# A linear-attention and two-MoE kernel: the first stage replanned with finer steps, and more mapping buffers

## The chip, the cores and the metric

The kernel runs on one core of one Trainium2 chip. The metric is the device time of one launch in microseconds (us), the median of the runs shown. The data is float32 throughout; matmuls are exact to float32 by splitting each operand into a high and a low part (three matmuls for one product).

## The reference

Three layers run one behind the other on 2304 tokens (4 batches of 576) of width 512 (8 heads of 64). A linear attention with 128 random features, a gated feed-forward layer ("MoE 1", inner width 1536), and a routed layer with 8 experts of which each token takes one ("MoE 2", inner width 1024).

```python
def phi(x):
    proj = np.einsum('bhsd,md->bhsm', x, omega)
    sq = np.sum(x * x, axis=-1, keepdims=True) / 2.0
    h = proj - sq
    h = h - np.max(h, axis=-1, keepdims=True)
    return np.exp(h) / np.sqrt(m)
q_p, k_p = (phi(q_s), phi(k_s))
kv = np.einsum('bhsm,bhsd->bhmd', k_p, v)
z = np.sum(k_p, axis=2)
num = np.einsum('bhsm,bhmd->bhsd', q_p, kv)
den = np.einsum('bhsm,bhm->bhs', q_p, z)[..., None] + 1e-06
attn = num / den
...
g = x @ w_gate
x2 = g * (1.0 / (1.0 + np.exp(-g))) * (x @ w_val) @ w_out
...
e_idx = np.argmax(x2 @ w_gate2 + modality_bias[modality_id], axis=1)
out[mask] = gate_w[mask, None] * (np.maximum(x2[mask] @ w1[e], 0.0) @ w2[e])
```

## The kernel before

The tokens are cut into 18 tiles of 128, and three tiles make one of six groups. A **unit** is the attention work of one tile and four heads, for k or for q. Its parts are named in `unit_stages`: T (transpose x on PE, tile `xt`), xh (copy to SBUF, ACT), xl (low part, VectorE), sq (squares), ss and sc (their sum and its scaling), pj (projection on PE, tile `pr`), rd (row maximum on VectorE, tile `mx`), md (two small subtractions on GpSimd, tile `mx` again), ex (exp on ACT, tile `h`). A k unit then adds to the sums kv (PE) and a q unit goes on with qt, qc, nm, dv, xt, hi, lo (transposed back, multiplied with kv, divided, and laid as high and low part into `xT`, the input of MoE 1).

MoE 1 takes a group in 12 steps f: 24 matmuls into `gv` for gate and value, an activation in five small steps (`th`, `uh`, `ul`), and nine matmuls into `acc`. Its weights come as 36 chunks (`wraw`), and in the first stage VectorE and ACT turn each chunk into a high and a low part in five steps (`wsteps`: one half-rate mask step, two combining steps, a cast on ACT, a subtraction).

The **first stage** runs from the start to the end of group 0 of MoE 1. It holds the first 16 units (10 of k, 6 of q, "start" units), the 14 units of the next group, all 36 chunks and the 12 steps f of group 0. The order in which this work is written out is set by a list scheduler, the class `Plan`: each step has an engine, a duration, what it needs, a rank and the buffers that it takes and gives. `run` picks the step that can start first and among equals the lowest rank, and calls its function, which records the instructions. Each engine later works off its own list in that order and waits where a step isn't ready. The durations stand in the table `dur`, the ranks come from constants at the top of the file (CR, CD, UR, MR and others). From group 1 on a clock of due times (`Tasks`) sets the order instead.

The routing of MoE 2 is found in rounds (`finish_route`). Its function `c` makes, per three tiles, three products `f_mv` and three one-hot tiles `f_lh` on VectorE, and PE multiplies them into `inv`. `f_lh` has three buffers in all, so the next three wait until PE has read the last ones. The pair `FR` sets how far apart these steps are due and how long after them their matmuls are.

In `s1b` the low part xl is recorded in the same step as xh, and in the plan this step is a step of ACT. The start units' vt memsets and copies, the scaling of ss and the sum of kv (`kv_put`) are likewise recorded inside other steps (first_edge, md, kv).

Of the kernel before, what the change touches and what calls it, by code (L numbers as in the profile page):

```python
# [29 lines left out]
FR = ((1.35, 3.0), (2.8, 6.0))  # L30
MD = (0, 0, 0.17, 1.8, 2.18)
QL = -0.4
QD = 0.51
LAT = 0.34
GRAIN = 0.02
CR = -13.06
CD = -7.43
CS = 11.68
UR = 67.55
UD = 9.05  # L40
MR = 44.82
MS = 30.96
RR = 91.36
XL = 19.61
WU = 4
GF = 0
# [3 lines left out]
RS = 3.38  # L50
PU = 14.29
# [29 lines left out]
class Plan:  # L81


    def __init__(self, bufs, lag):
        self.todo = []
        self.free = {}
        self.lag = lag
        self.bufs = {k: [0.0] * n for k, n in bufs.items()}
# [6 lines left out]
    def run(self, last):  # L95

        while last[7] is None:
            best = None
            for s in self.todo:
                eng, dur, fn, after, rank, take, give, end = s  # L100
                if any(a[7] is None for a in after) or any(not self.bufs[b] for b in take):
# [3 lines left out]
                key = (t // GRAIN, rank)  # L105
                if best is None or key < best[0]:
                    best = key, t, s
            key, t, s = best
            self.todo.remove(s)
# [3 lines left out]
            for b in s[6]:  # L113
                self.bufs[b].append(s[7] + LAT)
# [4 lines left out]
def kernel(  # L119
# [60 lines left out]
    with tc.manual_schedule():  # L180
# [76 lines left out]
        def load_v(n, vt):  # L257
            kind, t, j = units[n]
            if not edge(t):
                (r, m, b, s), = segs(t)  # L260
                nc.gpsimd.memset(vt[:, :, D:D + 2], 1.0)
                nc.sync.dma_start(out=vt[:, :, 0:D], in_=v[b, 4 * j:4 * j + 4, s:s + m, :].rearrange("h s d -> s h d"))
                return

            for hp in range(2):
                for i, (r, m, b, s) in enumerate(segs(t)):
                    nc.gpsimd.memset(vt[hp][r:r + m, :, 1 - i, :], 0.0)
                    nc.gpsimd.memset(vt[hp][r:r + m, :, i, D:D + 2], 1.0)
                    h = 4 * j + 2 * hp
# [3 lines left out]
        def pump():  # L273
            while nload[0] < len(units) and room["xin"]:
# [4 lines left out]
                nload[0] += 1  # L279
                pump_v()  # L280
            pump_v()
# [14 lines left out]

        def freed(tag):
            room[tag] += 1
            pump()
# [17 lines left out]
        def first_quad(src, j):  # L317
            quad[src, j] = wpool.tile([P, 4, 4, D], F32, tag="w", name="quad")
            nc.sync.dma_start(out=quad[src, j].rearrange("p h r d -> p h (r d)"),
                              in_=(k if src == "k" else v)[0, 4 * j:4 * j + 4, 0:4 * P, :].rearrange(  # L320
                                  "h (p r) d -> p h (r d)", r=4))
# [15 lines left out]
        def first_edge(j):  # L337
            n = units.index(("k", 4, j))
            vt = wpool.tile([P, 1024], F32, tag="w", name="vt")
            vt = [vt[:, 512 * a:512 * a + 4 * (D + 2)].rearrange("p (h b d) -> p h b d", h=2, b=2) for a in range(2)]  # L340
            loads[n] = first_x(n)
            vals[n] = vt
            load_v(n, vt)
# [8 lines left out]
        first_quad("k", 0)  # L352
        first_quad("v", 0)
# [81 lines left out]
        def unit_stages(i):  # L435
# [4 lines left out]
            native = start or i < n_start + min(GF, n_grp[0])  # L440
            accum = not start and i < n_start + n_grp[0]
# [8 lines left out]
            def s1():  # L450
# [5 lines left out]
                else:  # L456
                    x = loads.pop(i)
                    h = attn.tile([P, 4, M], F32, tag="h", name="h", bufs=2)
                    xh = attn.tile([P, 2, P], F32 if native else F32R, tag="xh", name="xh", bufs=1)
# [36 lines left out]
            def s2():  # L496
                xh, xl = st["xh"], st.get("xl")
                pr = st["pr"] = bank([P, 4, M], "pr")
                for a in range(2):
                    o = pr[:, 2 * a:2 * a + 2, :].rearrange("p h m -> p (h m)")  # L500
                    if native:
# [14 lines left out]
            def s2m():  # L516
                ss, mx = st["ss"], st["mx"]

                if start or accum:

                    if start:
                        nc.gpsimd.tensor_scalar(out=ss, in0=ss, scalar1=half_s2, scalar2=None, op0=ALU.mult)
# [23 lines left out]
            def s3k():  # L546
                h, vt = st["h"], vts.pop((t, j)) if x_none else vals.pop(i)
# [929 lines left out]
```

## Time and profile before

| | |
|---|---|
| median of three runs | 883.11 us (882.98 to 883.4) |
| the profiled execution, device time | 882.91 us |
| its span, first to last instruction | 880.7 us |
| PE busy | 854.5 us, 97% of the span |
| VectorE (DVE) busy | 598.9 us, 68% |
| ScalarE (ACT) busy | 370.4 us, 42% |
| GpSimd (POOL) busy | 97.1 us, 11% |

The span is 2.2 us shorter than the execution's device time. PE is the engine that sets the end: its matmuls of group 1 to the last expert follow each other almost without a gap, so a time that the first stage saves or loses moves everything behind it by the same amount. A share over the whole run says little of the first stage, where VectorE, GpSimd and ACT are as busy as PE.

### The profile page before, as it was taken

Reading aid. Unit: us, or ns where it says so; the run is one execution under the profiler, and the core shown is the slowest. Engines: PE = TensorE matmul, PEld = TensorE weight load, DVE = VectorE, ACT = ScalarE, POOL = GpSimd, SP = SyncE. Lnnn points to the kernel's source line nnn. Section 1 sums busy time; section 2 is a strip of 40 time slices with the busy share of each in tenths; the row PEclk is TensorE's granted clock in tenths of the full one; section 3 lists DMA queues with packets and bytes.
Section 4 is the critical chain, followed back from the end, with each engine's and each line's share of the span. In section 5 each row is a group of like instructions: output and inputs, shape, how many; then the busy total and the mean of one; then the engine's idle time right before and its main releaser. Section 6 shows DMA issues by size and latency. Waiting matters only on the chain. (4 is left out here: it accounts for less than half of the span.)

```text
span 880.7 us, 14618 instructions
## 1 busy us (share of the span) xinstructions
PE 854.5 (97%) x5115; PEld 789.1 (90%) x5115; DVE 598.9 (68%) x1582; ACT 370.4 (42%) x1023; POOL 97.1 (11%) x236
## 2 busy tenths in 40 slices
PE   7989999999999999999999999999999999999994
PEld 6878988999999999999999999999999999889994
DVE  5989999466665667555676665478787777876520
ACT  4865666343333433333433431111374445555420
POOL 6702101000000000000000000000112014311010
PEclk9999999999999999999999999999999999999998
DMA  8726642032223112141111311041767654666000
GB/s 268 210 67 203 190 152 78 7 114 55 61 60 103 42 42 55 43 127 47 36 37 44 84 31 42 33 135 31 266 216 282 199 180 149 237 236 238 28 27 26
DMA packets 89374, 98.69 MB, mean 112 GB/s; under 512 B 53488, under 2 KB 55554, under 8 KB 89291
## 3 DMA queue, kind: packets, MB, share of 16 engines
q1 hardware_dynamic: 85979, 87.90, 32.5%
q0 software_dynamic: 3040, 9.70, 3.2%
q8 instruction: 42, 0.69, 0.3%
q14 instruction: 41, 0.34, 0.1%
q10 hardware_dynamic: 272, 0.07, 0.0%
HBM read 84.26 MB, written 13.65 MB: 111 GB/s over the span
## 5 line engine op out<-in xcount | busy, mean ns | idle before, releaser
L166 PE MATMUL gv<-xT,w 128*128 128x384 f32 x576 | 202.2, 351 | 0.3 <-DVE th L1022 0.3
L168 PE MATMUL gv<-xT,w 128*128 128x384 f32 x576 | 194.8, 338 | 0.0
L167 PE MATMUL gv<-xT,w 128*128 128x384 f32 x576 | 194.5, 338 | 0.0
L166 PE MATMUL acc<-w,uh 128*128 128x512 f32 x352 | 143.5, 408 | 0.0
L168 PE MATMUL acc<-w,ul 128*128 128x512 f32 x352 | 139.1, 395 | 1.1 <-DVE ul L1201 1.0
L167 PE MATMUL acc<-w,uh 128*128 128x512 f32 x352 | 138.7, 394 | 0.0
L533 ACT ACTIVATE h<-pr,mx 128x128 f32<-128x128 f32 x224 | 64.0, 369 | 140.0 <-DVE mx L528 132.7
L166 PEld LDWEIGHTS gv<-xT,w 128*128 128x128 f32 x576 | 109.2, 190 | 4.2 <-DVE th L1022 1.4
L167 PEld LDWEIGHTS gv<-xT,w 128*128 128x128 f32 x576 | 109.2, 190 | 2.7
L168 PEld LDWEIGHTS gv<-xT,w 128*128 128x128 f32 x576 | 108.9, 189 | 0.0
L738 DVE SCALAR_TENSOR_TENSOR wge<-xrow,wge 128x512 f32<-128x512 f32 x144 | 98.6, 685 | 10.6 <-DMA wge<-wg2t 9.9
L172 DVE TENSOR_TENSOR w<-raw,w 128x512 fp32r<-128x512 f32 x128 | 85.1, 685 | 3.2 <-ACT w L171 2.3
L168 PEld LDWEIGHTS acc<-w,ul 128*128 128x128 f32 x352 | 66.0, 188 | 17.0 <-DVE ul L1201 2.4
L166 PE MATMUL h<-sx,w 128*128 128x256 f32 (+1 forms) x256 | 78.7, 308 | 0.0
L168 PE MATMUL h<-sx,w 128*128 128x256 f32 (+1 forms) x256 | 77.6, 303 | 0.0
L167 PE MATMUL h<-sx,w 128*128 128x256 f32 (+1 forms) x256 | 77.4, 302 | 0.0
L171 ACT CAST w<-raw 128x512 fp32r<-128x512 f32 x128 | 74.1, 618 | 2.4 <-DMA raw<-in_moe_w_dram 2.4
L167 PEld LDWEIGHTS acc<-w,uh 128*128 128x128 f32 x352 | 66.5, 189 | 7.5
L166 PEld LDWEIGHTS acc<-w,uh 128*128 128x128 f32 x352 | 66.4, 189 | 7.2
L1031 ACT CAST uh<-th 128x384 fp32r<-128x384 f32 x72 | 37.5, 521 | 72.7 <-DVE th L1026 72.5
L512 DVE TENSOR_REDUCE mx<-pr 128x4 f32<-128x512 f32 x72 | 49.4, 687 | 22.9 <-PE pr L168 19.8
L1022 DVE SCALAR_TENSOR_TENSOR th<-th,gv 128x384 f32<-128x384 f32 x72 | 39.6, 550 | 35.3 <-ACT th L1019 35.3
(232 smaller groups left out, 1404.2 us busy)
## 6 DMA issues: line engine op xcount, KB each, us to landing
raw<-in_moe_w_dram SPq DMA_DIRECT2D x64, 512.0 KB, 4.9
wge<-wg2t SPq DMA_DIRECT2D x48, 256.0 KB, 3.5
scr<-xrow SPq DMA_DIRECT2D x33, 256.0 KB, 3.0
wraw<-in_moe_w_gate_dram SPq DMA_DIRECT2D x12, 512.0 KB, 4.6
wraw<-in_moe_w_val_dram SPq DMA_DIRECT2D x12, 512.0 KB, 4.9
wraw<-in_moe_w_out_dram SPq DMA_DIRECT2D x12, 512.0 KB, 4.5
xin<-in_q_dram SPq DMA_DIRECT2D x26, 128.0 KB, 2.4
xin<-in_k_dram SPq DMA_DIRECT2D x24, 128.0 KB, 3.5
```

Source lines behind the costliest of these rows:

```text
L166: nc.tensor.matmul(o, lh, rh, start=start, stop=False, skip_group_check=True)
L167: nc.tensor.matmul(o, lh, rl, start=False, stop=False, skip_group_check=True)
L168: nc.tensor.matmul(o, ll, rh, start=False, stop=stop, skip_group_check=True)
L171: nc.scalar.copy(hi, src)
L172: nc.vector.tensor_tensor(out=lo, in0=src, in1=hi.bitcast(F32), op=ALU.subtract)
L512: nc.vector.tensor_reduce(out=mx, in_=pr, axis=AX.X, op=ALU.max)
L533: nc.scalar.activation(out=h[:, a, :], in_=pr[:, a, :], func=ACTF.Exp, bias=mx[:, a:a + 1])
L738: nc.vector.scalar_tensor_tensor(out=st[e][:, 1, :], in0=xrows[i], scalar=1.0, in1=st[e][:, 0, :], op0=ALU.mult, op1=ALU.mult, accum_out=L ...
L1022: nc.vector.scalar_tensor_tensor(out=th[f], in0=th[f], scalar=1.0, in1=ps.pop((f, "g")), op0=ALU.add, op1=ALU.mult)
L1031: nc.scalar.copy(u[f][0], th[f])
```

## The change

Work that was recorded inside other steps becomes steps of its own in the plan: xl (VectorE), sc (GpSimd), the edge units' vt memsets (GpSimd, ahead of their loads), the last sum of kv in a batch (`ka`, VectorE), and for the later k units the refill of the v buffer (`pv`, GpSimd). The lag between engines becomes a table by engine instead of one number, loads get a longer lag, durations are set anew, and so are nearly all ranks. The first load of k is cut into two halves, the transposition of the gate weights (`turn_gate`) waits for its load and the last value step, and the path `GF` that was switched off goes. In the routing, `f_lh` gets 8 buffers instead of 3, the due times `FR` are set anew, and `ge` of the third round, which runs only when tokens are left over, moves to another pool.

```diff
-FR = ((1.35, 3.0), (2.8, 6.0))
+FR = ((1.35, 2.6), (2.9, 4.0))
-LAT = 0.34
+LAT = dict(pe=0.25, act=0.14, dve=0.13, pool=0.14, dma=2.3)
-CR = -13.06
-CD = -7.43
+CR = 1.76
+CD = -8.74
...
-        first_quad("k", 0)
-        first_quad("v", 0)
+        first_quad("k", 0, 2)
...
             def s1b():
-                if native:
-                    nc.scalar.copy(st["xh"], st["xt"])
-                else:
-                    st["xl"] = attn.tile([P, 2, P], F32R, tag="xl", name="xl", bufs=1)
-                    split(st["xt"], st["xh"], st["xl"])
+                nc.scalar.copy(st["xh"], st["xt"])
+
+            def s1x():
+                xl = st["xl"] = attn.tile([P, 2, P], F32R, tag="xl", name="xl", bufs=1)
+                nc.vector.tensor_tensor(out=xl, in0=st["xt"], in1=st["xh"].bitcast(F32), op=ALU.subtract)
...
+            def s1e():
+                nc.gpsimd.tensor_scalar(out=st["ss"], in0=st["ss"], scalar1=half_s2, scalar2=None, op0=ALU.mult)
...
-                if t == own[-1]:
-                    kv_put((b, j), kv_ps[0], slice(0, 4))
                 if not x_none:
                     freed("vin")
+                if not planned and t == own[-1]:
+                    s3p()
+
+            def s3p():
+                kv_put(segs(t)[0][2:3] + (j,), kv_ps[0], slice(0, 4))
...
         def freed(tag):
             room[tag] += 1
-            pump()
+            if tag == "xin" or not planning:
+                pump()
...
-                        lh[i] = t_("f_lh", [P, P], F32R, bufs=GT)
+                        lh[i] = t_("f_lh", [P, P], F32R, bufs=8)
...
-        dur = dict(T=0.34, xh=0.26, sq=0.7, ss=0.42, pj=0.87, rd=0.7, md=0.4, ex=1.01, kv=0.83, ko=0.42, kw=0.43,
-                    kp=0.42, qt=0.43, qc=0.39, nm=0.87, dv=1.09, xt=0.22, hi=0.27, lo=0.34)
+        dur = dict(T=0.22, xh=0.26, xl=0.34, sq=0.57, ss=0.33, sc=0.55, pj=0.87, rd=0.6, md=0.5, ex=1.02, kv=0.83,
+                   ka=0.35, pv=0.25, ko=0.18, kw=0.43, kp=0.18, qt=0.43, qc=0.48, nm=0.84, dv=0.75, xt=0.22, hi=0.26, lo=0.34)
...
-            got["edge", j] = plan.add("dma", 1.46, lambda j=j: first_edge(j), rank=-8 + 4 * j, take=["w", "w"])
+        for j, rank in enumerate((KE, KF)):
+            s = plan.add("pool", 1.2, lambda j=j: first_edge(j, True), rank=rank, take=["w"])
+            got["edge", j] = plan.add("dma", 2.0, lambda j=j: first_edge(j, False), [s], rank=rank, take=["w"])
...
-        plan.add("pe", 0.4, turn_gate, [], MR + 75)
+        plan.add("pe", 0.6, turn_gate, [loaded, half["v", 1]], MR + 75)
```

What the new ranks do to the order is seen in the program's own lists. From group 1 of MoE 1 to the end the lists of all engines are the same before and after, but for where the routing's steps stand among the work around them.

PE, the last rows of the start units and the first matmuls of MoE 1 (`xot` brings a q unit's result back, `gv` is MoE 1, `pr<-om_h` the projection of a unit of the next group, `wt` is `turn_gate`); before:

```order
L605 MATMUL xot<-ident,first 128x128 x2
L470 MATMUL xt<-ident,xin 128x128 x2
L695 MATMUL wt<-ident,wg_97 8x128 x4
L166 MATMUL pr<-om_h,xh 128x256
L167 MATMUL pr<-om_l,xh 128x256
L168 MATMUL pr<-om_h,xl 128x256
L166 MATMUL pr<-om_h,xh 128x256
L167 MATMUL pr<-om_l,xh 128x256
L168 MATMUL pr<-om_h,xl 128x256
L166 MATMUL gv<-xT_644,w 128x384
L167 MATMUL gv<-xT_645,w 128x384
```

and of the change, in the same place:

```order
L653 MATMUL xot<-ident,first 128x128 x2
L514 MATMUL xt<-ident,xin 128x128 x2
L187 MATMUL gv<-xT_634,w 128x384
L188 MATMUL gv<-xT_635,w 128x384
L189 MATMUL gv<-xT_634,w 128x384
L187 MATMUL gv<-xT_634,w 128x384
L188 MATMUL gv<-xT_635,w 128x384
L189 MATMUL gv<-xT_634,w 128x384
L187 MATMUL pr<-om_h,xh 128x256
L188 MATMUL pr<-om_l,xh 128x256
L189 MATMUL pr<-om_h,xl 128x256
```

Before, the projections of two units and `wt` stand ahead of the first `gv`; now the first six `gv` come at once behind the last `xot`, both projections come later, and `wt` has gone to the end of group 0.

ACT, from the four copies of the first start units on (`first<-pr,mx` is the exp of a unit, `w<-wt` the cast of a weight chunk, `first<-xt` the copy xh of a start unit); before:

```order
L476 COPY first<-xt 128x256 x4
L533 ACTIVATE first<-pr,mx 128x128 x4
L476 COPY first<-xt 128x256
L533 ACTIVATE first<-pr,mx 128x128 x4
L420 CAST w<-wt 128x512
L533 ACTIVATE first<-pr,mx 128x128 x4
L420 CAST w<-wt 128x512
```

and of the change:

```order
L519 COPY first<-xt 128x256 x4
L578 ACTIVATE first<-pr,mx 128x128 x4
L464 CAST w<-wt 128x512
L578 ACTIVATE first<-pr,mx 128x128 x4
L464 CAST w<-wt 128x512
L519 COPY first<-xt 128x256 x2
L578 ACTIVATE first<-pr,mx 128x128 x4
```

The first two casts have each moved ahead of an exp, and the copy of the first edge unit, which stood behind the first exp, now stands behind the second cast.

PE, late in the run, at the fifth `inv` of the second routing round (`h` and `acc` are an expert's matmuls, `gx` transposes gathered rows); before:

```order
L168 MATMUL acc_8787<-w,ul 128x512
L1159 MATMUL gx<-ident,grow 128x128 x4
L166 MATMUL h_8932<-sx_8517,w 128x256
L167 MATMUL h_8932<-sx_8518,w 128x256
L168 MATMUL h_8932<-sx_8517,w 128x256
L166 MATMUL h_8932<-sx_8517,w 128x256
L167 MATMUL h_8932<-sx_8518,w 128x256
L168 MATMUL h_8932<-sx_8517,w 128x256
L974 MATMUL inv<-f_mv,f_lh 128x18 x3
```

and of the change:

```order
L189 MATMUL acc_8791<-w,ul 128x512
L1211 MATMUL gx<-ident,grow 128x128 x4
L1026 MATMUL inv<-f_mv,f_lh 128x18 x3
L187 MATMUL h_8933<-sx_8518,w 128x256
L188 MATMUL h_8933<-sx_8519,w 128x256
L189 MATMUL h_8933<-sx_8518,w 128x256
```

The three `inv` matmuls stand six matmuls earlier.

## Rows read from the trace of the kernel before

**Rows 1.** The page, part 1: busy time, share of span, instructions by engine

```profile
PE 854.5 (97%) x5115; PEld 789.1 (90%) x5115; DVE 598.9 (68%) x1582; ACT 370.4 (42%) x1023; POOL 97.1 (11%) x236
```

**Rows 2.** Stretch: its us, busy PE, PEld, DVE, ACT, POOL, granted clock, DMA

```profile
0.00:58.70 58.70, 47.72 (x290) 40.31 (x291) 46.52 (x106) 38.96 (x133) 32.22 (x110) 1.00 0.66 193
58.70:168.50 109.80, 106.91 (x651) 98.34 (x650) 96.68 (x203) 62.62 (x224) 13.76 (x34) 0.97 0.43 133
168.50:760.00 591.50, 591.50 (x3528) 553.20 (x3527) 398.25 (x1147) 223.57 (x574) 33.86 (x76) 1.00 0.32 99
760.00:785.00 25.00, 23.85 (x158) 20.97 (x157) 17.28 (x53) 11.73 (x24) 2.86 (x3) 1.00 0.56 199
```

**Rows 3.** Waits of PE, 0 to 150 us: total us, times, longest

```profile
PE kv L555 <- ACT h L533: 1.4, 1, 1.4
...
PE wt L695 <- DVE xl L172: 1.2, 1, 1.2
...
PE gv L166 <- DVE th L1022: 0.3, 1, 0.3
```

**Rows 4.** Busy time by stretch, around two falls of the clock

```profile
53.00:58.90 5.90, 3.26 (x22) 2.48 (x23) 5.71 (x14) 4.07 (x23) 0.45 (x2) 1.00 0.50 134
58.90:62.30 3.40, 3.40 (x12) 3.40 (x11) 3.34 (x7) 1.66 (x5) 0.77 (x2) 0.51 0.55 158
86.90:88.30 1.40, 0.02 (x1) 0.00 (x1) 0.61 (x2) 0.42 (x2) 0.87 (x2) 1.00 0.14 56
89.60:93.10 3.50, 3.50 (x15) 3.24 (x14) 3.50 (x8) 2.24 (x9) 0.08 (x1) 0.51 0.30 67
```

**Rows 5.** Timeline at the seam: start us, us, engine, instruction [idle before]

```profile
57.05 0.41 DVE L613 TENSOR_TENSOR xT<-xot,xT 128x256 fp32r<-128x256 f32 x1
...
57.88 0.39 PE L166 MATMUL pr<-om_h,xh 128*128 128x256 f32 x1 [0.69 <-ACT h L533]
...
58.70 0.34 PE L166 MATMUL gv<-xT,w 128*128 128x384 f32 x1
```

**Rows 6.** Timeline ahead of the stall at 87 us, GpSimd

```profile
85.31 2.26 POOL L523 TENSOR_TENSOR mx<-ss,mx 128x4 f32<-128x4 f32 x1 [4.58 <-ACT w L420]
```

**Rows 7.** GpSimd's first subtraction: min/median/max ns, first and last start

```profile
L523 POOL TENSOR_TENSOR mx<-ss,mx x30: 200/202/2256, 10.2 to 149.9; 128x4 f32<-128x4 f32 x30
```

**Rows 8.** VectorE groups of the first stage: busy us, mean ns, idle before

```profile
L411 DVE SCALAR_TENSOR_TENSOR wt<-wraw,wt 128x512 int32<-128x512 int32 x36 | 25.1, 704 | 0.0
...
L512 DVE TENSOR_REDUCE mx<-pr 128x4 f32<-128x512 f32 x30 | 20.4, 681 | 2.8 <-PE pr L502 2.7 <-PE pr L168 0.2
L407 DVE TENSOR_SCALAR wt<-wraw 128x512 int32<-128x512 int32 x36 | 15.3, 437 | 0.0
...
L507 DVE TENSOR_REDUCE ss<-first 128x4 f32<-128x256 f32 x16 | 6.5, 409 | 1.5 <-POOL vt L331 0.9 <-POOL first L484 0.6
L172 DVE TENSOR_TENSOR xl<-xt,xh 128x256 fp32r<-128x256 f32 x14 | 5.9, 419 | 3.0 <-ACT xh L171 2.9
```

**Rows 9.** Timeline of the start units

```profile
10.79 0.79 PE L470 MATMUL xt<-ident,quad 128*128 128x128 f32 x4
...
11.65 0.42 DVE L407 TENSOR_SCALAR wt<-wraw 128x512 int32<-128x512 int32 x1
...
13.48 1.15 ACT L533 ACTIVATE first<-pr,mx 128x128 f32<-128x128 f32 x4
...
14.49 0.64 ACT L420 CAST w<-wt 128x512 fp32r<-128x512 f32 x1
...
17.33 0.37 ACT L533 ACTIVATE first<-pr,mx 128x128 f32<-128x128 f32 x1 [2.19 <-POOL mx L524]
```

**Rows 10.** Waits at the second routing round, 760 to 785 us

```profile
DVE f_lh L969 <- PE inv L974: 7.5, 5, 3.0
```

**Rows 11.** The DMA view: one issue, KB each, median us to landing

```profile
wge<-wg2t SPq DMA_DIRECT2D x48, 256.0 KB, 3.5
...
quad<-in_k_dram SPq DMA_DIRECT2D x2, 512.0 KB, 5.1
```

More of the change, by code (lines that the diff above doesn't have):

```diff
@@ L85, in __init__ @@
         self.todo = []
+        self.next = {}
         self.free = {}
@@ L95, in run @@
     def run(self, last):
+        left = {}
+        ready = []
+        self.next = {}
+        for n, s in enumerate(self.todo):
+            wait = {id(a) for a in s[3] if a[7] is None}
+            for a in wait:
+                self.next.setdefault(a, []).append((n, s))
+            left[id(s)] = len(wait)
+            if not wait:
+                ready.append((n, s))
         while last[7] is None:
             best = None
-            for s in self.todo:
+            for n, s in ready:
                 eng, dur, fn, after, rank, take, give, end = s
-                if any(a[7] is None for a in after) or any(not self.bufs[b] for b in take):
+                if any(not self.bufs[b] for b in take):
                     continue
@@ L108, in run @@
             key, t, s = best
+            ready.remove((key[2], s))
             self.todo.remove(s)
@@ L113, in run @@
             for b in s[6]:
-                self.bufs[b].append(s[7] + LAT)
+                self.bufs[b].append(s[7] + self.lag[s[0]])
+            for n, x in self.next.get(id(s), ()):
+                left[id(x)] -= 1
+                if not left[id(x)]:
+                    ready.append((n, x))
             s[2]()
@@ L268, in load_v @@
                     nc.gpsimd.memset(vt[hp][r:r + m, :, i, D:D + 2], 1.0)
+        def load_v(n, vt, memset=True):
+            kind, t, j = units[n]
+            if memset:
+                ones_v(n, vt)
+            if not edge(t):
+                (r, m, b, s), = segs(t)
+                nc.sync.dma_start(out=vt[:, :, 0:D], in_=v[b, 4 * j:4 * j + 4, s:s + m, :].rearrange("h s d -> s h d"))
+                return
+            for hp in range(2):
+                for i, (r, m, b, s) in enumerate(segs(t)):
                     h = 4 * j + 2 * hp
@@ L279, in pump @@
                 nload[0] += 1
+                if not planning:
+                    pump_v()
+            if not planning:
                 pump_v()
-            pump_v()
         def pump_v():
@@ L439, in unit_stages @@
             start = i < n_start
-            native = start or i < n_start + min(GF, n_grp[0])
-            accum = not start and i < n_start + n_grp[0]
+            planned = i < n_start + n_grp[0]
+            accum = not start and planned
             def bank(shape, name):
@@ L625, in unit_stages @@
                 parts.update(kv=s3k)
+                if planned and t == max(x for x in batch_tiles(segs(t)[0][2]) if not edge(x)):
+                    parts.update(ka=s3p)
             else:
@@ L1304 @@
         on.update(sq="pool", ss="dve", md="pool")
[L1305 removed]
+        needs.update(ss=["sq"], sc=["ss"], rd=["pj"], md=["rd", "sc"], ex=["md"])
         ready = []
@@ L1308 @@
         om_split = plan.add("act", 0.3, lambda: split(om_f, om_h, om_l), [], OR)
-        pumped = plan.add("dma", 1.6, pump, [got["edge", 1]], PU)
+        pumped = plan.add("dma", 1.6, lambda: (pump(), pump_v()), [got["edge", 1]], PU)
         for i in range(nu):
@@ L1325 @@
                 step["x"] = got["edge", j]
-            native = i < n_start + min(GF, n_grp[0])
-            for n, f in unit_stages(i).items():
+            parts = unit_stages(i)
+            if kind == "k" and not early:
+                parts["pv"] = pump_v
+            for n, f in parts.items():
                 d = 0.43 if n == "kv" and edge(t) else dur[n]
@@ L1362 @@
         ra, rb, rc, rd = route_setup()
-        s = plan.add("dma", 0.5, later_loads, [s], XL)
+        s = loaded = plan.add("dma", 0.5, later_loads, [s], XL)
         s = plan.add("dve", 0.14, ra, [s], RR)
```

133 lines of the change are left out of this document (79 added, 54 removed).

## The prediction

> **What bounds the kernel now.** I read the page's busy times first, then the busy time by stretch, then who waited for whom on PE, and last the timeline at the places where PE waited. The page says that PE is busy 97% of the span [rows 1]. By stretch the picture is sharper: from 168.5 us, where group 1 of MoE 1 begins, to 760 us PE has not one idle microsecond, and VectorE has a third of its time free [rows 2]. What an order could still gain there is nothing. The idle time of PE lies in three places: 58.70 - 47.72 = 11.0 us before the first `gv` matmul, 109.80 - 106.91 = 2.9 us between it and 168.5 us, and 25.00 - 23.85 = 1.15 us around the second routing round [rows 2]. To this the clock adds something in the second stretch: its mean is 0.97, because of two falls of some 3.4 us each to 0.51, that is from 2.4 to 1.2 GHz [rows 4]. At half clock such a fall costs half its length, 1.7 us. Ahead of the first fall PE was busy 3.26 of 5.90 us, ahead of the second it had stood still for 1.4 us [rows 4].
>
> So the change can gain at most the avoidable part of 11.0 us, 2.9 + 3.4 = 6.3 us behind it, and 1.15 us late. What stands against it: PE's work in the first stage is the same before and after, and VectorE's nearly so. Both engines are close to full between 90 and 150 us, so a reordering gains only where one of them really stood.
>
> The sum is made against the profiled execution, 882.9 us (span 880.7 and 2.2 around it), 0.2 us under the median of the three runs. A measurement here tells about 0.2%, 1.8 us, from no change.
>
> **The change part by part.**
>
> *Start of the plan, up to some 20 us.* The edge units' memsets on GpSimd move to the first microseconds, where GpSimd is free; before, the second set stood in the way of a vt memset that VectorE waited 0.9 us for [rows 8]. That is a gain of at most 0.9 us. Against it, on ACT two weight casts have moved ahead of exps. Before, the second exp began at 13.48 and the first cast at 14.49 us [rows 9]. Now that cast is first. It can't start before VectorE's third step of the chunk, which in the new list has three steps in front of it behind the start at 11.65 us [rows 9] that the chunk work has in both orders; by the durations 0.44 + 0.70 + 0.44 + 0.70 less overlap this is 13.7 to 13.8 us [rows 8]. The exp then begins near 14.4, 0.9 us later, and the copy of the edge unit behind the second cast puts that unit's projection 1.6 us later. ACT then stood idle for 2.19 us before the third exp anyway [rows 9], so some of it is taken up. Bounds -0.9 and +1.6; I take 0, since VectorE has its list full of ready chunk steps in either order.
>
> *The first k load in two halves.* A load of 512 KB landed 5.1 us after issue, one of 256 KB 3.5 us after [rows 11]. The first half can't help the first transposes, which stand behind the random features' own load. The second half is needed by units 2 and 3, whose transposes, in their turn on PE, began at 10.79 us [rows 9], so 2 x 3.5 - 5.1 = 1.9 us more would be hidden: 0. The Trainium skill, "DMA: Bandwidth & Descriptors", section "Anatomy of one DMA", speaks against the cut: each DMA has a fixed cost of about 2 us whatever its size. By that rule the second half would land some 2 us later, which the same cover hides.
>
> *The seam at 58.7 us.* Before, PE waited 1.2 us for its `wt` transposes behind an xl [rows 3] and 0.69 us for an exp [rows 5], and of the last 5.9 us it idled 2.6 [rows 4]. In the new list the first six `gv` stand right behind the last start unit, both projections come later and `wt` much later. The last high/low part of a start unit ended at 57.46 us and the first `gv` came at 58.70 [rows 5]: 1.2 us to gain. Three things go against it. The two projections are PE work that is now done after the first `gv`, where PE has no idle time: 58.70 - 57.88 = 0.8 us each [rows 5], 1.6 in all. The last high/low part also stands later in VectorE's new list. I counted the rows in front of it: one weight chunk more (0.44 and three times 0.70) and six small setup steps of some 0.2, less two xl of 0.42 and one `mx` of 0.68 [rows 8] and some overlap, 1.2 to 1.7 us. And the clock's fall at 58.9 us, 1.7 us, may go if PE no longer idles there. -1.2 + 1.6 + 1.5 - 1.7 = +0.2. Bounds: -2.9 (no extra VectorE delay, the projections find idle time) and +3.1 (the clock still falls, and the exp still comes late). I take 0.
>
> *The stall at 87 us.* PE stood 1.4 us for a k unit's exp [rows 3], and behind it came the second fall of the clock, 1.7 us [rows 4]. The exp had waited for GpSimd's two tiny subtractions, of which the first took 2.26 us [rows 6], against 0.20 us at its median [rows 7]. Before, GpSimd's list also held the v buffers' memsets in front of such steps; as `pv` they are now steps with a place of their own, and xl, of 0.42 us on VectorE [rows 8], is now in the plan, which before counted it to ACT. So a meeting of just this kind should not come again in this place: -3.1 us. Bounds -3.1 and 0. But by the program's lists the PE work between a projection and the matmul that needs its exp has shrunk, from 4.8 to 3.9 us in the mean over 14 units, so I add one wait for an exp of the size of that at the seam, 0.7 us [rows 5]. Together -2.4.
>
> The Trainium skill, "GPSIMD Engine Reference", section "Specifications", says that GpSimd shares its SBUF interfaces with VectorE and is held up by VectorE instructions with two SBUF inputs or in a two-port mode. The 2.26 us fell among such instructions. By that rule the new plan, which books a fixed 0.5 us, meets the same chance wherever chunk steps follow a row maximum; that is the second rival below.
>
> *VectorE's load by step f.* Ahead of the end of step 4 its new list holds some 2.6 us less work, ahead of step 9 some 3 us less, at steps 5 to 7 the same. PE waited only 0.3 us in all for these steps [rows 3], so this is cover and no gain: 0. If PE came earlier by more than 3 us, VectorE would be late next.
>
> *`turn_gate` at the end of group 0.* The same four transposes, one copy and one load that the gate loads of group 0 need; these stand behind it in SP's list as before, and 591 us without an idle PE follow [rows 2]: 0.
>
> *Mapping buffers and FR.* VectorE waited five times, 7.5 us in all, for PE to read `f_lh` [rows 10]; the stretch has 1.15 us of idle PE [rows 2]. With eight buffers three new tiles needn't wait for three old ones. The matmuls are due 2 us earlier after their VectorE steps, but still 4 us after them, against some 1.1 us of work. -1.1 us; bounds -1.5 (with the slower first matmuls after a wait) and 0.
>
> Sum: 0 + 0 + 0 - 2.4 + 0 + 0 - 1.1 = -3.5, so 882.9 - 3.5 = **879.4 us**.
>
> **The rivals.**
>
> 1. *Everything after the seam closes.* Both falls of the clock and the 2.9 us of idle PE go: -6.3, with the mapping -1.1: 875.5 us. For it: xl and the sums of kv were missing in the old plan. Against it: the tighter distances.
>
> 2. *No gain in the first stage.* The finer plan is still no picture of the chip: GpSimd's steps stretch by chance (0.20 to 2.26 us, [rows 7]), so a stall of the old size comes elsewhere, and only the mapping's 1.1 us stays: 881.8 us, no change by the bound above. This also covers that the change doesn't do what it says.
>
> 3. *Slower: the start comes late.* The casts ahead of exps shift the start units by 1.6 us, the last high/low part is 1.5 us later by its place, the two projections' 1.6 us fall into full PE time, less 1.2 us at the seam; the stall and the falls stay as they are. +1.6 + 1.9 - 1.1 = +2.4: 885.3 us. It decides from the point where the first `gv` starts later than about 59.9 us: with the 1.6 us of work put off and the mapping's gain this is +1.7 us. For it: the first `gv` waits for the last start unit in any order, and the planner prices PE at full speed from its first matmul on. Against it: VectorE had steps ready in the start.
>
> **How the numbers follow.** The forecast's case has a chance of 0.44, rival 1 0.14, rival 2 0.24, rival 3 0.18. Faster by over 0.2%: 0.44 + 0.14 = 0.58; within 0.2%: 0.24; slower: 0.18. The likeliest case has 877 to 881.3 us for itself. The range that holds the time 8 times in 10 goes from 875.5, with half of rival 1 below it, to 885.0, with somewhat over half of rival 3 above it.
>
> **What would show it.** In the profile of the changed kernel: the wait of `wt` for xl gone; no half clock near 59 and 90 us; PE's idle time behind the first `gv` under 2.9 us; group 1 beginning some 2.4 us earlier, at 166; VectorE's wait for `inv` at 760 to 785 us gone and PE there without a gap. The first `gv` should start between 57.5 and 59 us. It is wrong if `gv` starts after 60 us, if PE waits for exps more than 2 us in the group's stretch, if the clock falls two or more times there, or if PE waits for `f_lh` in the routing.

## The result and the profile after

The changed kernel takes 873.3 us (median of 4 runs, 873.20 to 873.81) against 883.2 us before (882.98 to 883.40, 4 runs): a ratio of 0.9889, 95% interval 0.9872 to 0.9906. The forecast was 879.4 us, with a range from 875.5 to 885.0. The sign was right; the gain, 9.9 us, was almost three times the 3.5 forecast, and the time lies below the range.

The page's busy times, and the same four stretches as [rows 2], cut at the changed kernel's own first `gv` (54.58 us), start of group 1 (160.71 us) and second routing round:

```profile
PE 851.5 (98%) x5115; PEld 788.1 (90%) x5115; DVE 599.1 (69%) x1581; ACT 369.3 (42%) x1024; POOL 101.0 (12%) x236
```

```profile
0.00:54.58 54.58, 46.80 (x272) 39.56 (x272) 44.94 (x105) 36.34 (x115) 35.05 (x108) 0.97 0.71 212
54.58:160.71 106.13, 105.33 (x667) 97.48 (x668) 96.71 (x203) 63.88 (x245) 14.45 (x36) 1.00 0.44 135
160.71:751.00 590.29, 590.17 (x3520) 552.17 (x3519) 397.77 (x1142) 222.87 (x572) 32.34 (x75) 1.00 0.32 99
751.00:776.00 25.00, 25.00 (x169) 22.85 (x169) 19.75 (x63) 12.63 (x26) 4.21 (x3) 1.00 0.62 211
```

The kernel before, cut in the same way at the weight loads of its first `gv` and of group 1:

```profile
0.00:58.58 58.58, 47.60 (x289) 40.19 (x290) 46.40 (x106) 38.96 (x133) 32.22 (x110) 1.00 0.66 193
58.58:168.54 109.96, 107.07 (x652) 98.50 (x651) 96.80 (x204) 62.62 (x224) 13.76 (x34) 0.97 0.43 133
```

The span went from 880.7 to 871.3 us, 9.4 us less. So 58.58 - 54.58 = 4.0 us were gained ahead of the first `gv` and 109.96 - 106.13 = 3.8 us between it and group 1. The other 1.6 us came behind the start of group 1. PE's idle time fell from 11.0 to 54.58 - 46.80 = 7.8 us in the start, from 2.9 to 106.13 - 105.33 = 0.8 us beside MoE 1, and from 1.15 us to nothing in the second routing round. Over the whole first stage that is 5.3 of the 7.8 us; the other 2.5 us are less busy time for the same work. Beside MoE 1 only VectorE is nearly as full as PE (96.7 of 106.1 us); ACT has 63.9 and GpSimd 14.5 us of work there, less than the text ahead says of the first stage as a whole.

What PE waited for in the first stage:

```profile
PE pr L546 <- ACT first L578: 2.1, 1, 2.1
PE pr L546 <- ACT first L519: 1.8, 2, 1.2
PE omT L412 <- POOL vt L287: 1.2, 1, 1.2
...
PE kv L600 <- ACT h L578: 0.5, 1, 0.5
```

The wait of `wt` for xl and the 1.4 us of kv behind an exp [rows 3] are gone, and so are both falls of the clock of [rows 4]. New are a wait of 2.1 us in the start and a fall of the clock behind it. Which falls an execution shows differs between executions of the same lists, as the last section tells, so they are not put down to the change here. The place in the start:

```profile
26.40:28.50 2.10, 0.01 (x1) 0.00 (x0) 1.74 (x4) 1.87 (x7) 1.86 (x5) 0.99 1.15 339
28.50:31.90 3.40, 3.39 (x8) 2.75 (x9) 2.69 (x5) 2.68 (x10) 2.96 (x8) 0.50 1.11 321
```

### The profile page after: what moved, and what is told of

It reads as the page before. It is cut to its first block, busy times and chain, and to the rows that moved or that the text cites. A ratio compares the mean times of both kernels' runs of the same rounds, so it can differ in the third digit from the quotient of the medians.

```text
span 871.3 us, 14616 instructions
## 1 busy us (share of the span) xinstructions
PE 851.5 (98%) x5115; PEld 788.1 (90%) x5115; DVE 599.1 (69%) x1581; ACT 369.3 (42%) x1024; POOL 101.0 (12%) x236
```

## The experiments

Where an experiment moves single steps (e6, e7, e8), the planner's order was written out as a list of step numbers, and the entries in question moved in that list: a few at one place in e7 and e8, the steps of the whole seam in e6. The first column of the table is the start of the first `gv` (its weight load) in the profiled execution, the second that of group 1; PE's idle time in the two stretches is their length less PE's busy time in them. Two profiled kernels that leave the first stage of before as it was (e2, e3) started group 1 at 168.86 and 169.15 us, so differences under some 0.6 us in these columns tell nothing. The runs were made in several sets, and the kernel before, run again in each, had medians from 883.1 to 883.8 us; the ratios are against the same set. Between two variants of the changed kernel, whose ratios have intervals of 0.0015 to 0.0025 to either side, a difference of 1 or 2 us in the median is therefore taken as real only where the start of group 1 moved with it.

| kernel | first gv | group 1 | PE idle to gv | PE idle gv to group 1 | median us |
|---|---|---|---|---|---|
| before | 58.58 | 168.54 | 11.0 | 2.9 | 883.2 |
| changed | 54.58 | 160.71 | 7.8 | 0.8 | 873.3 |
| before + e5 k in halves | 58.22 | 168.84 | 9.2 | 5.1 | 882.4 |
| before + e6 seam order | 55.22 | 169.99 | 9.9 | 5.9 | 885.7 |
| before + e7 gv ahead of kv | 59.10 | 169.74 | 10.2 | 3.9 | 883.5 |
| before + e12 md on VectorE | 58.80 | 169.78 | 10.5 | 5.3 | 884.5 |
| changed, e4 k whole | 55.80 | 160.95 | 9.2 | 0.0 | 874.1 |
| changed, e19 k in quarters | 53.80 | 159.90 | 6.6 | 0.8 | 871.9 |
| changed, e8 exp ahead | 54.28 | 160.44 | 8.2 | 0.8 | 873.3 |
| changed, e10 memsets late | 55.01 | 161.14 | 8.5 | 0.8 | 873.8 |
| changed, e11 md on VectorE | 54.17 | 163.25 | 7.6 | 2.2 | 876.2 |
| changed, e14 sums on ACT | 57.71 | 163.83 | 10.2 | 0.8 | 876.5 |
| changed, e15 division on ACT | 54.26 | 162.29 | 8.2 | 1.6 | 874.8 |
| changed, e13 one rank moved | 54.22 | 163.42 | 8.0 | 3.7 | 876.0 |
| changed, e17 old group ranks | 55.31 | 162.68 | 7.9 | 2.0 | 875.3 |
| changed, e18 old start ranks | 56.72 | 164.49 | 9.4 | 1.3 | 877.0 |
| changed, e9 all ranks old | 57.01 | 168.66 | 8.9 | 4.7 | 880.9 |

### The mapping: e1, e2, e3

```diff
 e1, on the changed kernel (e3, on the kernel before, is the reverse)
-FR = ((1.35, 2.6), (2.9, 4.0))
+FR = ((1.35, 3.0), (2.8, 6.0))
-                        lh[i] = t_("f_lh", [P, P], F32R, bufs=8)
+                        lh[i] = t_("f_lh", [P, P], F32R, bufs=GT)
 e2, on the kernel before: only bufs=8 (e2 and e3 also take the new place of ge, which makes the room)
```

> The changed kernel with the old mapping: three f_lh buffers and the old FR. Behind 556 us the changed kernel gained 1.9 us, where 1.1 was forecast. Theory M: all of it is the mapping, the 1.15 us of idle PE and some 0.8 us of matmuls that ran slower around it: 873.3 + 1.9 = 875.2 us, and PE has some 1.1 us idle again in the second routing round. Rival: the mapping is worth the forecast's 1.1 us and the rest is the place at which the round falls: 874.4 us. Second rival: VectorE's waits for inv were cover: 873.3 us.

> The kernel before with eight f_lh buffers (and ge of the third round in the other pool, which makes the room), FR as it was. Theory M1: the buffers alone take away VectorE's five waits for inv (7.5 us) and with them PE's idle time: 883.2 - 1.9 = 881.3 us. Rival: the matmuls are still due 6 us behind their VectorE steps, so what matters is FR: 883.2 us.

> The kernel before with eight f_lh buffers and the new FR, the first stage as it was. Theory M: the mapping's gain stands by itself, 883.2 - 1.9 = 881.3 us, no PE idle time between 760 and 785 us. Rival: it shows only where the first stage is early: 883.2 us.

Measured: e1 875.0 us (874.57 to 875.67), 1.7 us over the changed kernel; e2 881.3 us (ratio 0.9981, 0.9971 to 0.9991), 1.9 us under before; e3 882.1 us (0.9987, 0.9978 to 0.9996). In e1, around the second routing round, the old waits are back:

```profile
DVE f_lh L1021 <- PE inv L1026: 7.5, 5, 3.0
PE acc L189 <- DVE ul L1253: 1.0, 2, 0.8
```

```profile
752.70:777.70 25.00, 23.82 (x157) 20.87 (x156) 17.26 (x53) 11.72 (x24) 2.40 (x3) 1.00 0.58 198
```

and in e2 they are gone:

```profile
760.00:785.00 25.00, 25.00 (x170) 22.84 (x169) 19.27 (x63) 12.19 (x27) 3.65 (x4) 1.00 0.61 206
```

So the eight buffers by themselves take away the waits; the new FR adds nothing that can be told. By the medians this part is worth 1.1 us (e3) to 1.9 us (e2), and e2's interval, for one, goes from 0.8 to 2.6 us; by the profiles, the time from the start of group 1 to the end is 1.6 to 2.4 us shorter with eight buffers. PE's 1.18 us of idle time in the routing round can be only part of that; where the rest lies was not traced.

### The first k load: e4, e5, e19

```diff
 e4 (e19 puts 4 where the changed kernel has 2; e5 brings the halves to the kernel before)
-        first_quad("k", 0, 2)
+        first_quad("k", 0)
```

> The changed kernel with the first k load in one piece of 512 KB. In the changed kernel the first transpose of the random features started at 4.31 us, before at 5.29. Theory L: the big load was in the way of the features' load, so in one piece both land 1.0 us later and all of it stays: omT at 5.3 us, the first gv at 55.6, 873.3 + 1.0 = 874.3 us. Rival: VectorE has steps enough, and the 1.0 us is taken up before the first gv: 873.3 us. Second rival: the earlier start has another cause (the v load, the memsets), and omT stays at 4.3 us.

> The kernel before with the first k load in two halves and nothing else. Theory L: the random features and the first half of k land 1.0 us sooner (the first transpose of the features at 4.3 instead of 5.29 us); the first gv comes 1.0 us sooner, 57.6 us. What is left of it at the end: in the changed kernel the whole load cost 0.8 us in all, so 882.4 us. Rival: VectorE's order behind it takes it up: 883.2 us.

> The changed kernel with the first k load in four pieces of 128 KB instead of two of 256. Theory L: the features' load shares the engines with less data ahead of it and lands some 0.3 to 0.5 us sooner, the first transposes need two of the pieces: the first transpose of the features at 3.9 us, the end 873.0 us. Rival: PE waits at 4.3 us for something else by now, or the two issues more cost what they give: 873.3 us or 0.5 more.

The first transpose of the random features (`omT`), in the timelines of e4, of the changed kernel and of e19:

```profile
5.86 0.45 PE L412 MATMUL omT<-ident,om 128*128 128x128 f32 x1 [2.72 <-DMA om<-in_omega_dram]
```

```profile
4.31 0.45 PE L412 MATMUL omT<-ident,om 128*128 128x128 f32 x1 [1.17 <-POOL vt L287]
```

```profile
3.31 0.45 PE L412 MATMUL omT<-ident,om 128*128 128x128 f32 x1 [0.17 <-DMA om<-in_omega_dram]
```

The features' own load of 64 KB, on ACT's queue, is the same in all three; what differs is the size of the pieces on SyncE's queue. In the changed kernel the wait is put down to a memset that happened to end then; in e19 PE went on at 3.31 us, a microsecond before those memsets end. In e5, on the kernel before, `omT` began at 4.29 instead of 5.29 us. So with a piece of half the size the small load was there 1.0 us (e5) and 1.55 us (e4) sooner, and with a quarter 1.0 us sooner again. What was left at the end: e4 874.1 us (873.73 to 874.67), by the median 0.8 us slower than the changed kernel, which the intervals (0.9885 to 0.9914 against 0.9872 to 0.9906) don't tell apart; e5 882.4 us, ratio 0.999 (0.998 to 1.0), not to be told from before. e4 came to its first `gv` 1.2 us late and made up 1.0 us of it beside MoE 1, where PE did not wait at all.

e19 took 871.9 us (871.67 to 873.43), ratio 0.9873 (0.9857 to 0.9889). It beats the kernel before clearly. Against the changed kernel its median is 1.4 us lower, and the profile shows group 1 0.8 us sooner. But the two intervals overlap, and the profiled execution, in which group 1 was sooner, was itself the slowest of e19's four, at 873.43 us. So the second step is likely but not settled.

### One place at a time on the kernel before: e6, e7, e12

```diff
 e6, PE's order at the seam
-pr x6   xot x2   xt x2   wt x4   pr x6   gv x12 ...
+xot x2   gv x6   pr x6   gv x6   xt x2   gv x6   pr x6 ...   (wt at the end of group 0)
 e7, PE's order at 87 us
-gv x6   kv x4   pr x6   gv x6
+gv x6   gv x6   kv x4   pr x6
 e12 (and e11 on the changed kernel), for the units beside MoE 1
+            def md_(e=nc.gpsimd if start else nc.vector):
...
-                    nc.gpsimd.tensor_tensor(out=mx, in0=ss, in1=mx, op=ALU.subtract)
-                    nc.gpsimd.tensor_tensor(out=mx, in0=mx, in1=ss, op=ALU.subtract)
+                    e.tensor_tensor(out=mx, in0=ss, in1=mx, op=ALU.subtract)
+                    e.tensor_tensor(out=mx, in0=mx, in1=ss, op=ALU.subtract)
```

> The kernel before with the steps at the seam in the changed kernel's order: the first two halves of gv right behind the last start unit, the projections of the next two units behind them, the gate's transposes at the end of group 0; all else stays. Theory S: the waits of 1.21 and 0.69 us go, the first gv comes some 2.2 us sooner (56.4 us), 1.7 us of PE work moves behind it, and the clock does not fall at 59 us (1.7 us): group 1 and the end 2.2 us sooner, 881.0 us. Rival V: what comes behind is paced by VectorE's weight chunks, so the early gv waits later: 883.2 us. Second rival: the clock falls at 59 us all the same: 882.7 us.

> The kernel before with one PE step moved: six gv matmuls of step f = 3, whose weights and buffer are there, go ahead of the kv that stood 1.4 us for its exp at 87 us. Theory P (the stall term of the prediction): the idle time there shrinks by the 1.0 us of these matmuls, the fall of the clock at 89.7 us (1.7 us) goes, and both reach the end: 883.2 - 2.7 = 880.5 us. Rival V: VectorE, which is full from 89 to 157 us, sets the pace, and group 1 begins where it did: 883.2 us. Between: only the idle time goes and the clock falls: 882.2 us.

> The kernel before with the same move of md to VectorE. Theory G: no held subtraction, so neither PE's 1.4 us at 87 us nor the same thing at 96 us, where it came in the runs that missed the first, and no fall of the clock between 85 and 100 us: 1.4 + 1.7 us less, some of it eaten by 2.0 us more on VectorE: 881.5 us (880.1 to 882.5). Rival V: VectorE's list sets the pace, so the stage ends where it did or 1 us later: 883.5 us.

All three took away the wait that they aimed at, or most of it, and gained nothing. e6 had its first `gv` at 55.22 us, 3.4 us sooner, and was slower in the end (885.7 us, ratio 1.0031, 1.0018 to 1.0043). Its projections were later now, and PE stood for exps instead; its waits from 55 to 170 us begin:

```profile
PE kv L555 <- ACT h L533: 3.4, 2, 2.3
PE xot L605 <- DVE first L596: 1.8, 1, 1.8
```

e7 (883.5 us, 1.0003, 0.9992 to 1.0014) cut PE's stand at 87 us from 1.4 to 0.3 us. Right behind it, at 91 us, PE stood 1.8 us for an activation step of VectorE (`th`), and behind that the clock fell, at 94.2 us:

```profile
PE gv L166 <- DVE th L1022: 2.0, 2, 1.8
```

GpSimd's subtraction was held again too, and longer than before, but in this place PE had other work and did not wait for it:

```profile
96.64 3.12 POOL L523 TENSOR_TENSOR mx<-ss,mx 128x4 f32<-128x4 f32 x1 [3.52 <-DVE mx L512]
```

e12 (884.5 us, 1.0007, 0.9998 to 1.0017) left GpSimd out of these units. No subtraction was held and no exp made PE wait, but the 28 added instructions, some 162 ns each where 70 had been priced, stood in VectorE's list, and PE waited for the activations instead, 58 to 170 us:

```profile
PE gv L166 <- DVE th L1022: 3.8, 4, 1.6
```

### One place at a time on the changed kernel: e8, e10, e11, e14, e15

```diff
 e8, ACT's order at 26 us
-copy of kv   weight cast   exp of unit 6
+exp of unit 6   copy of kv   weight cast
 e10, first_edge: the memsets in the load's step again
-                load_v(n, vals[n], False)
+                load_v(n, vals[n], True)
...
-            ones_v(n, vt)
 e15, s4b, for the q units beside MoE 1
+                if accum:
+                    for h in range(4):
+                        nc.scalar.activation(out=st["x"][:, h, :], in_=num[:, h, 0:D], func=ACTF.Copy, scale=den[:, h, :])
+                    return
```

e14 lets ACT square and sum for the q units of the start, as `s1c` does for the later units, and drops `ss` and `sc` there.

> The changed kernel with one ACT step moved: the exp of start unit 6, for whose buffer PE stood 2.1 us at 26.4 us with the clock at half for 3.4 us behind it, goes ahead of a copy of kv that waited for VectorE and of a weight cast. Theory C: the exp starts 0.9 us sooner, PE stands 1.2 us; if the clock then holds, the first gv comes 0.9 + 1.7 us sooner less what VectorE can't follow, 52 to 54 us, and the end 1 to 2.6 us sooner: 871.5 us (870.7 to 872.3). Rival V: VectorE bounds the start, the first gv stays at 54.6 us: 873.3 us. Second rival: the clock falls all the same: 872.5 us.

> The changed kernel with the memsets of the two edge units recorded again in the step of their loads instead of in steps of their own ahead of them; the order of all else stays. The second set then stands later in GpSimd's list, where it stood before. Theory: this is the prediction's bound of 0.9 us at the start, VectorE's wait for a vt memset; the first gv 0.9 us later and some of it left at the end, 874.0 us. Rival: GpSimd has time there and nothing waits: 873.3 us.

> The changed kernel with the two small subtractions of md on VectorE, right behind the row maximum, for the 14 units beside MoE 1 (28 instructions more on VectorE, 28 fewer on GpSimd; the start units keep GpSimd). Theory G: GpSimd's subtraction was held while VectorE ran instructions with two SBUF inputs back to back (2.66 us at 90.7 us); without it VectorE's 2.19 us of idle time at 93 us goes, and the exps come 0.5 to 2 us sooner. Price: 28 instructions of some 0.07 us, 2.0 us of VectorE. If VectorE paces the stage, that is 2.2 - 2.0: 873.1 us (872.3 to 874). Rival P: PE's waits alone count, of which 0.5 us hang on it: 872.8 us. Second rival: the added VectorE work delays the chunks more than it saves: 875 us.

> The changed kernel with the squares and their sums of the 6 q units of the start on ACT (as the later units have them) instead of squares on GpSimd, the sum on VectorE and its scaling on GpSimd; the order stays. VectorE has 6 x 0.34 = 2.0 us less work ahead of the first gv, ACT, idle 10 us between 13 and 54.6 us, some 5.8 us more. Theory V: the first gv comes up to 2.0 us sooner (52.6 to 54 us), the end 871.9 us. Rival A: ACT is in the way of the exps of these units, and the first gv stays or comes later: 873.3 to 874.5 us.

> The changed kernel with the last step of the division (num times 1/den) of the 6 q units beside MoE 1 on ACT, four instructions a unit, instead of one on VectorE; the order stays. VectorE issues one every 0.34 us there, so it has 6 x 0.34 = 2.0 us less work; ACT, busy 64 of 106 us there, has some 6 us more. Theory V: VectorE paces the first stage, so group 1 starts 1.5 to 2 us sooner (158.7 to 159.2 us) and the end comes at 871.5 us. Rival P: PE's work paces it (0.8 us idle left): 873.3 us at best, later where ACT delays an exp.

In e8's profile the clock stayed up through the place where it had fallen:

```profile
26.40:31.90 5.50, 3.44 (x15) 2.49 (x16) 4.72 (x10) 5.03 (x18) 4.87 (x11) 1.00 1.08 305
```

and gained 0.3 us at the first `gv` and nothing at the end (873.3 us, 872.17 to 874.24). In e10 too the clock did not fall there, and its first `gv` was 0.4 us later (873.8 us). So 3.4 us at half clock in the start cost next to nothing here.

e11 (876.2 us), e14 (876.5 us) and e15 (874.8 us) were all slower, and their group 1 came later by 2.5, 3.1 and 1.6 us. e11 had 4.0 us more of VectorE work beside MoE 1. But work taken off VectorE did not pay either: the exps, casts and copies that stand behind the added ACT work came later. In e15 VectorE, with six instructions fewer, waited for ACT's xh 3.1 us (2.2 in the changed kernel) and for ACT's part of `xT` 1.6 us between 95 and 154 us:

```profile
DVE xl L523 <- ACT xh L519: 3.1, 2, 2.2
DVE xT L665 <- ACT xT L662: 1.6, 3, 0.9
```

So e14 and e15 give no support to the theory that VectorE alone paces the first stage. They don't rule it out, since each put onto ACT what it took off VectorE; no run takes work off VectorE and adds none elsewhere. The theory that PE's single waits pace the stage fell with e6, e7 and e12.

### Model or order: e9, e13, e17, e18

All four keep the finer steps, durations and lags of the changed kernel, and change constants of the ranks only.

```diff
 e13
-UR = 86.72
+UR = 89.72
 e17: UR 67.55, UD 9.05, MR 44.82, MS 30.96, RR 91.36, as before
 e18: CR -13.06, CD -7.43, CN 1.4, CS 11.68, RS 3.38, PU 14.29, QL -0.4, QD 0.51, XL 19.61, as before;
      KA, KB, KC, KE, KF: -9, -5, -5, -8, -4, as the old formulas give
 e9: both
```

> The changed kernel with the ranks of the kernel before (new ranks that had none take the old formulas' values): the finer planner without the new search over ranks. Theory R: the planner's finer steps and lags are worth most of the first stage's 7.8 us by themselves, as they see VectorE and GpSimd: 876 us (874 to 878). Rival: the ranks were fitted to the old model, and with another model they give some other order, no better than before: 881 us or more (with the mapping's 1.9 us in it).

> The changed kernel with one rank constant of the units beside MoE 1 (UR) at 89.72 instead of 86.72, model and all else the same; the planner writes another order from about the seam on. Theory R: the finer model by itself makes good orders, so this one is within 1 us: 873.3 to 874.3 us. Rival F: the gain lies in one fitted order, and a neighbour gives most of the group's part (some 3.8 us) back: 875 to 877 us.

> The changed kernel with the old ranks of the work beside MoE 1 (UR, UD, MR, MS, RR), the new ones for the loads, the chunks and the start units. Theory F (one fitted order): the first gv comes at 54 to 55 us, since the start's ranks are new, but the stretch behind it is as long as before, 110 us, so group 1 starts at 164.5 us and the end is 873.3 + 3.8 = 877.1 us (875.5 to 879). Rival R: the finer steps alone keep PE full beside MoE 1: 873.3 to 874.3 us.

> The changed kernel with the old ranks of the loads, the chunks and the start units (CR, CD, CS, QL, QD, RS, PU, XL and the old formulas' values for the rest), the new ones beside MoE 1. Theory F: the first gv comes at 57 us, as with all old ranks, and the new ranks beside MoE 1, fitted to other chunk ranks, don't bring the stretch under 109 us: group 1 at 166 us, the end 878.5 us (876 to 881). Rival: the two halves stand by themselves, and only the start's 2.4 us are lost: 875.7 us.

With all old ranks (e9) group 1 began at 168.66 us, 0.1 us later than before: the finer model alone gained nothing in the first stage. The 880.9 us (ratio 0.9964, 0.9952 to 0.9976) are 2.1 to 4.2 us under before; the profile has 1.9 us of it behind the start of group 1, which is what the mapping gives, and the rest isn't placed. One rank constant moved by 3 (e13) gave back 2.7 us at group 1, with the same first `gv`. The old ranks beside MoE 1 (e17) cost 2.0 us at group 1, those of the start (e18) 3.8 us, and both together 8.0. Read the other way round, from e9 on, the start's new ranks alone bring 6.0 of the 8.0 us and those beside MoE 1 alone 4.2: either half does much of the work without the other, and what they give overlaps. What was not tried is the old model with the new ranks, and which of the finer steps (xl, sc, pv, ka, the lags) the good order needs: each of them makes the planner write another order.

## Why the prediction was wrong

*The start, forecast 0 (-0.9 to +1.6).* With the seam, this is the step that failed: the first `gv` was expected between 57.5 and 59 us and came at 54.58, 4.0 us sooner than before, with 3.2 us less of idle PE ahead of it. The prediction set VectorE's full list against any gain there. But VectorE stood 58.70 - 46.52 = 12.2 us ahead of the first `gv` [rows 2], of which 2.5 us went (54.58 - 44.94 = 9.6), and its busy time there shrank by 1.6 us. Taken back one at a time, the cut of the k load costs 1.2 us at the first `gv` (e4) and the start's ranks 2.1 us (e18); at group 1 they cost 0.2 and 3.8 us. Which step of the new order does it was not singled out. The memsets, the only gain that was priced, cost 0.4 us at the first `gv` when put back (e10), which is within the noise. The delays that were priced against the change came smaller: the second exp began at 13.72 us where 14.4 was forecast, and the copy behind the second cast made PE wait 1.2 us (the second row of its waits above). PE's 2.1 us, from 26.4 us on, are another exp behind a copy and a cast, in a place that the prediction did not name; e8 shows that undoing it gains nothing.

*The first k load, forecast 0.* The failing sentence is that the first half can't help because the first transposes stand behind the features' own load. That load was what the halves helped: 1.0 us (e5), 1.55 us (e4). The rule of fixed cost that was cited against the cut, from the Trainium skill, "DMA: Bandwidth & Descriptors", section "Anatomy of one DMA", is measured there on loads that GpSimd issues. These are issued by SyncE, and with four pieces the first transpose of the features came another 1.0 us sooner (e19). The same page, section "Queues, rings and completion order", says that each DMA engine takes turns between the queues packet by packet. By that rule alone the size of the pieces on SyncE's queue would not matter to a small load on ACT's; here it did, 5.86, 4.31 and 3.31 us, and the measurement decides. Why it mattered was not tried.

*The seam, forecast 0 (-2.9 to +3.1).* The waits for `wt` and for the exp went as foreseen, and the profile shows no fall of the clock at 59 us. The count of rows that put the last low part 1.2 to 1.7 us later was no measure: that part ended at 54.87 us, 2.6 us sooner than before [rows 5]. e6 shows that the seam's order by itself brings the first `gv` 3.4 us forward and is still no gain at the end. So an early first `gv` alone proves nothing, and how the 4.0 us divide between start and seam stays open.

*The stall at 87 us, forecast -2.4.* Beside MoE 1 PE's idle time fell by 2.1 us and its busy time by 1.7 us, though it had 15 matmuls more there: 3.8 us shorter. The reason given was wrong, though. The same meeting came again, longer, in the changed kernel:

```profile
90.48 0.68 DVE L467 TENSOR_TENSOR w<-wt,w 128x512 fp32r<-128x512 f32 x1
90.70 2.66 POOL L568 TENSOR_TENSOR mx<-ss,mx 128x4 f32<-128x4 f32 x1 [2.28 <-DVE mx L560]
91.08 0.68 DVE L459 SCALAR_TENSOR_TENSOR wt<-wraw,wt 128x512 int32<-128x512 int32 x1
91.68 0.68 DVE L455 SCALAR_TENSOR_TENSOR wt<-wraw,wt 128x512 int32<-128x512 int32 x1
92.28 0.42 DVE L451 TENSOR_SCALAR wt<-wraw 128x512 int32<-128x512 int32 x1
92.62 0.68 DVE L459 SCALAR_TENSOR_TENSOR wt<-wraw,wt 128x512 int32<-128x512 int32 x1
...
93.67 1.14 ACT L578 ACTIVATE h<-pr,mx 128x128 f32<-128x128 f32 x4 [3.52 <-POOL vin L281]
94.09 1.21 PE L600 MATMUL kv<-vin,h 128*128 128x65 f32 x8 [0.51 <-ACT h L578]
95.49 0.42 DVE L523 TENSOR_TENSOR xl<-xt,xh 128x256 fp32r<-128x256 f32 x1 [2.19 <-ACT xh L519]
```

That much of the second rival was right. PE stood 0.51 us for it instead of 1.4: it had more to do in front of that kv. Of the 2.4 us, 1.7 were the price of a fall of the clock at half its length. No run shows that price at the end: e8 and e10 lose a fall and gain nothing, and e3, with the first stage of before, had one fall in place of two, none of them at 90 us, and began group 1 no sooner (169.15 us).

*`turn_gate`, forecast 0.* Right: from group 1 on PE has 0.1 us of idle time up to 751 us, as the third stretch shows.

*The mapping, forecast -1.1.* The mechanism was right. The term was perhaps too small: the medians give 1.1 to 1.9 us, the profiles 1.6 to 2.4, with the upper end set at 1.5.

The sum failed above all because it went place by place, and gave the places where no single wait was large (the start, the seam) nothing; what the runs show there in its place is that the new ranks, taken together, are worth 8.0 us at group 1 (e9). The first rival had the right direction, and missed the start as well. Of the signs named, the first `gv` and group 1 (160.7 us, not 166) came sooner than said; the others came true, but for one wait of 0.9 us of VectorE for `inv`.

## What to carry to other kernels

A list order in which several engines are nearly full is worth what it is worth as a whole, and its parts don't add up: two halves of the new ranks gave 6.0 and 4.2 us alone and 8.0 together. Three repairs of visible waits gained nothing one at a time, because the time came back as another wait further down the same lists; so a new order's gain couldn't be summed here from the waits of the old one, in either direction, and its range should reach to all the idle time of the stage that is not forced. A planner's model and its fitted ranks are one thing: a finer model with old ranks was worth 0 here, and a neighbouring rank lost a third of the first stage's gain. And look at what stands beside a small load that everything waits for: cutting the big one beside it let the small one through 1.0 to 1.55 us sooner and is a change of one number, though what was left at the end (0.7 to 0.8 us) is not clear of the noise.

## What the runs showed of the hardware

GpSimd's subtraction on 128x4 takes 0.20 us [rows 7], and in the longest cases was held for as long as VectorE went from one instruction to the next without a gap: 2.66 us through the five chunk instructions above, 3.12 us in e7. Four of the five have two SBUF operands; the fourth, the mask step (L451), has one, and the subtraction did not get through beside it either. It ended within 0.1 us of the moment at which VectorE ran out of ready work. The Trainium skill, "SBUF — State Buffer", section "SBUF: two separate sides", says of the port pair that VectorE and GpSimd share that whoever starts first has it for the whole instruction and the other is blocked, for VectorE instructions with two SBUF inputs or in a two-port mode. The trace agrees that the subtraction stood still; that the one blocked can lose several turns in a row, as here, is more than that. In the rows above the effect closes a circle: VectorE runs ahead through its ready steps, so GpSimd is held, so the exp is late, so VectorE's next step (xl) waits 2.19 us. What the hold costs at the end no run shows, since taking the subtraction off GpSimd gave VectorE more work (e11, e12).

Falls of TensorE's clock to half, 3.4 us each, are not the same in two executions of the same lists, and cost nothing here that can be told. e1 has the first stage of the changed kernel; in its profile the clock fell twice in the start, where the changed kernel's fell once, and group 1 began at 160.69 against 160.71 us. e3 has the first stage of before, with one fall against two, and group 1 began at 169.15 against 168.54 us. The stretches up to the first `gv` and from there to group 1, of e1 and then of e3 (the clock is the third number from the end):

```profile
0.00:54.62 54.62, 46.90 (x272) 39.93 (x273) 44.93 (x105) 36.60 (x115) 35.22 (x108) 0.94 0.70 212
54.62:160.69 106.07, 105.28 (x666) 97.45 (x667) 96.67 (x203) 63.80 (x245) 14.39 (x36) 1.00 0.44 135
0.00:58.94 58.94, 47.59 (x289) 40.13 (x289) 46.45 (x106) 38.95 (x133) 32.50 (x110) 1.00 0.66 191
58.94:169.15 110.21, 106.54 (x653) 97.05 (x652) 96.87 (x204) 62.44 (x224) 14.42 (x34) 0.98 0.43 132
```
